# Linear attention with a gated causal convolution: gated values of three batches held, output chunks kept within a batch

## The chip, the core and the metric

The kernel runs on one core of one Trainium2 chip. The metric is the device time of one launch in microseconds, lower is better. Everything is computed in float32; the three weights arrive as float64 and are narrowed on the core.

## The reference

```python
# q, k, v: (8, 8, 576, 64); g_norm: (64,); w_val, w_out: (512, 512); conv_w: (5, 512)
kv  = einsum('bhsd,bhse->bhde', k, v)
out = einsum('bhsd,bhde->bhse', q, kv)
x   = out / sqrt(mean(out*out, -1) + 1e-6) * g_norm
x   = x.transpose(0, 2, 1, 3).reshape(8, 576, 512)
gate_pre = sum(conv_w[t] * xp[:, t:t+576] for t in range(5))   # xp: x with 4 zero tokens ahead
gate = 1 / (1 + exp(-gate_pre))
result = (gate * (x @ w_val)) @ w_out                           # (8, 576, 512)
```

## The kernel before

The work goes batch by batch. For each batch of 576 tokens there are these stages, each made of small steps:

- Loads on SP's queue: `load_half` brings k and v, each in two halves of 512 KB (tiles k0, k1, v0, v1) for 512 tokens; `load_tails` brings the last 64 tokens of both; `load_q` brings q in four parts, each by four DMAs (batches 0 and 1: `load_q_rows`, three parts). Tiles k0, k1, v0 and v1 have two buffers each and q has four.
- `kv_product` sums k by v of each head on PE with 64 stationary columns, alternating between the two halves of a bank; `kv_copy` brings the result to `kvbd`.
- q is turned: on PE and ACT for batches 0 and 1 (`turn_q_rows`, `sort_q`), on DVE for later ones (`turn_q`, which frees the buffer of that part of q).
- `raw_product` makes the attention output in chunks of 128 tokens (the last of 64), ACT squares it (`square`), DVE sums (`sums`, tile `ss`), POOL takes the power -1/2 (`powers`, tile `rt`), DVE multiplies (`normalise`, tile `x`).
- x is turned to channels by tokens (`xT`): on PE and ACT for batches 0 and 1 (`turn_x`, `keep_x`), by DVE blocks and POOL's DMAs for later ones (`turn_blocks`, `move_blocks`). `halo` fills the four tokens ahead.
- Gates: ACT starts (`gate_start`), four taps on DVE (`gate_tap`), a sigmoid on ACT (`gate_end`), for each of four groups of channels.
- Values: `val_product` for batches 0 to 3; for batches 4 to 7 `val_fast`, seven products of half size in place of eight, with sums by `x_sums`, `val_sums` and `val_keep`. The results go to the tile `gv`, and `gated` multiplies the gate into them.
- Outputs: two batches are a pair `i` with 1152 tokens in `gv`, which are nine chunks of 128. Chunks are taken two at a time, `p` = 0 to 3, as seven products of half size (`fast_product`, with `token_sums` and `weight_sums` on DVE, `fast_keep` on ACT and DVE). `single` plans the ninth chunk, which is the last 128 tokens of the pair's second batch, with four matmuls of 512 columns (`out_product`, `keep_out`). `store` writes each chunk by four DMAs on SP's queue from one of three `ot` buffers.

In `gv` there is room for two batches, batch `b` at tokens `b % 2 * 576`. So in pair `i` the outputs with `p` = 0 and 1 use tokens 0 to 511, all of the first batch, and `p` = 2 and 3 use tokens 512 to 1023, of both batches.

The order of the instructions on each engine is fixed when the program is built. Each step is given to a `Planner` with an engine, a duration, a wanted time, the results it needs, and rings of buffers that it takes and frees. The planner always places the step that can start first, by its own durations; each engine runs its steps in this order and waits for what they need. A wanted time is `want` plus an entry of the table `SHIFTS`, a hand of time per kind of step and batch. `by_batch` rings, `gv` among them, are taken in the order of the batches. `narrow_weight` steps narrow each weight in slices (5 on DVE, 3 on ACT) out of the ring `w64`; `keep_warm` puts small matmuls on an identity into PE's gaps in the first 60 us of the plan.

```python
"k0": 2, "k1": 2, "v0": 2, "v1": 2, "tails": 2, "q": 4, ... "gv": 2, "ot": 3,
...
t = step["want"] - step["ahead"]
...
key = (max(t, now), step["want"], step["at"])
```

Of the kernel before, what the change touches and what calls it, by code (L numbers as in the profile page):

```python
# [9 lines left out]
FP32 = mybir.dt.float32  # L10
# [8 lines left out]


SHIFTS = {
    "fast_keep": {2: -131.5},
    "fast_product": {0: 9, 1: 19.5, 2: -23, 3: -0.5},
    "gate_start": {6: 11},
    "gate_tap": {1: 52.5, 2: 75, 3: 66, 4: 61.5, 5: 66.5, 6: 72, 7: 72},
    "halo": {5: 35},
    "keep_out": {1: 24},
    "kv_product": {6: 43.5},
    "load_half": {("k", 4): -9, ("k", 6): -68, ("v", 1): 15, ("v", 4): 7.5, ("v", 5): 18.5, ("v", 6): 14.5,
        ("v", 7): 20.5},  # L30
    "load_q": {3: -18, 4: 21.5, 5: 3, 6: -8, 7: 3.5},
    "load_q_rows": {1: 30},
    "load_tails": {3: 12.5},
    "move_blocks": {6: 43},
    "narrow_weight": {("wout", 1): -35, ("wout", 3): -172.5, ("wval", 3): 17},
    "normalise": {5: 12, 6: 12, 7: -28},
    "raw_product": {4: 1, 5: 6, 6: -15, 7: -18.5},
    "sort_q": {1: -88},
    "stage_weight": {("cw", 0): -273.5, ("wout", 0): 13, ("wout", 1): -186.5, ("wval", 0): -297.5,
        ("wval", 2): -5},  # L40
    "sums": {4: 48},
    "turn_blocks": {4: 36.5},
    "turn_q": {2: 36.5, 3: 16.5, 6: 9.5},
    "turn_q_rows": {1: 5.5},
    "turn_x": {1: 55.5, 7: -7},
    "val_fast": {5: -9, 7: 12},
    "val_product": {0: 3, 1: 54.5},
    "val_sums": {3: 32.5},
    "weight_sums": {2: 28},
}  # L50


# [85 lines left out]
def kernel(  # L138
# [50 lines left out]
    HB = P // TB  # L189
    NV = 2  # L190
    SV = S // NV
    S2 = 2 * S
    TURNED = 2
    TURNED_X = 2
    FAST_VAL = range(4, B)
    GATES = 3
    assert NJ == 4 and NB == 18
    assert 2 * T == P and NB * TB == S and SV <= 512 and C <= 512 and D == 2 * TB

# [6 lines left out]
    def ps(kind, shape, name):  # L206
        return psum.tile(shape, FP32, tag=kind, bufs=BANKS[kind], name=name)

    plan = Planner({
        "k0": 2, "k1": 2, "v0": 2, "v1": 2, "tails": 2, "q": 4, "w64": 3, "y": 1, "wexp": 2,  # L210
        "kv": 1, "kvbd": 2, "qT": 2, "tp": 1, "raw": 2, "mm": 4, "sq": 2, "ss": 3, "rt": 3,
        "x": 2, "xT": 2, "gate": GATES, "xs": 4, "gv": 2, "ot": 3,
    }, by_batch=("tails", "kvbd", "xT", "gv"))


# [3 lines left out]
    ident = const.tile([P, P], FP32, name="ident")  # L219
    mhalf = const.tile([P, H], FP32, name="mhalf")  # L220
    xTs = [const.tile([P, NK, SX], FP32, name=f"xT{i}") for i in range(2)]
    gv = const.tile([P, NK, S2], FP32, name="gv")

    sqs = [const.tile([P, H, D + 1], FP32, name=f"sq{i}") for i in range(2)]
    squared = []
# [30 lines left out]
    st = {}  # L256

    def load_half(name, src, b, i):
        t = loads.tile([P, H // 2, NJ, D], FP32, tag=f"{name}{i}", name=f"{name}{i}_{b}")
        nc.sync.dma_start(  # L260
            out=t[:].rearrange("p h j d -> p h (j d)"),
            in_=src[b, i * H // 2:(i + 1) * H // 2, 0:SF, :].rearrange(
                "h (p j) d -> p h (j d)", j=NJ),
        )
        st[name, b, i] = t
# [4 lines left out]
                out=tails[b % 2][n][0:T], in_=src[b, :, SF:S, :].rearrange("h s d -> s h d"))  # L270

    def load_q(b, hp):
        t = loads.tile([P, NB, D], FP32, tag="q", bufs=4, name=f"q{b}_{hp}")
        run = S // TB * D - TB
        flat = t[:].rearrange("p n d -> p (n d)")
        for half in range(2):
            for r in range(2):
                first = (2 * r + half) * TB
                nc.sync.dma_start(
                    out=flat[first:first + TB, 0:run],  # L280
                    in_=q[b, 2 * hp + r].rearrange("(t n) d -> t (n d)", t=TB)[
                        :, half * TB:half * TB + run],
                )
        st["q", b, hp] = t

    def load_q_rows(b, i):

        t = loads.tile([P, NB, D], FP32, tag="q", bufs=4, name=f"q{b}_{i}")
        t = t[:].rearrange("p n d -> p (n d)")
        if i < 2:  # L290
            t = t[:, 0:H // 2 * NJ * D]
            nc.sync.dma_start(
                out=t.rearrange("p (h a) -> p h a", h=H // 2),
                in_=q[b, i * H // 2:(i + 1) * H // 2, 0:SF, :].rearrange(
                    "h (p j) d -> p h (j d)", j=NJ),
            )
            st["q", b, i] = t.rearrange("p (h j d) -> p h j d", h=H // 2, j=NJ)
        else:
            t = t[0:T, 0:C].rearrange("p (h d) -> p h d", h=H)
            nc.sync.dma_start(out=t, in_=q[b, :, SF:S, :].rearrange("h s d -> s h d"))  # L300
            st["q", b, i] = t
# [287 lines left out]
        st["val", b, jt, n] = val  # L589

    def keep_val(b, jt, n):
        first = b % 2 * S + n * SV
        nc.scalar.copy(out=gv[:, jt, first:first + SV], in_=st["val", b, jt, n][:])  # L593

    def gated(b, jt):
        both = gv[:, jt, b % 2 * S:(b % 2 + 1) * S]
        nc.vector.tensor_tensor(out=both, in0=both, in1=st["gate", b, jt][:], op=ALU.mult)  # L597


# [37 lines left out]

    def val_keep(b, mj, n):
        a, b_, c = (st[bank, "val", b, mj][:] for bank in "abc")
        to = lambda o, half: gv[:, mj + 2 * o, b % 2 * S + half * SV:b % 2 * S + (half + 1) * SV]  # L640
        add = lambda out, one, two: nc.vector.tensor_tensor(out=out, in0=one, in1=two, op=ALU.add)
        if n == 0:
            nc.scalar.copy(out=to(0, 0), in_=a)
        elif n == 1:
            nc.scalar.copy(out=to(1, 1), in_=c)
        elif n == 2:
            nc.scalar.copy(out=to(0, 1), in_=a)
        elif n == 3:
            add(to(0, 0), b_, to(0, 0))
        elif n == 4:  # L650
            add(to(1, 1), a, to(1, 1))
        elif n == 5:
            add(to(0, 1), c, to(0, 1))
        else:
            nc.scalar.copy(out=to(1, 0), in_=a)

    rows_out = out.rearrange("b (t n) c -> b n t c", n=NB)

    def out_product(i, c):
        po = ps("mm", [P, C], f"out{i}_{c}")  # L660
        for jt in range(NK):
            nc.tensor.matmul(  # L662
                po[:], gv[:, jt, c * P:(c + 1) * P], wout[:, jt, :],
                start=(jt == 0), stop=(jt == NK - 1),
            )
        st["po", i, c] = po

    def keep_out(i, c):
# [11 lines left out]
    def token_sums(i, h, n):  # L680

        if n % 2 == 0:
            st["sums", i, h, n // 2] = loads.tile(
                [P, 2, NK // 2, 2, P], FP32, tag="w64", bufs=3, name=f"sums{i}_{h}_{n}")
        block = lambda r, k: gv[:, k, h * SF:(h + 1) * SF].rearrange(
            "p k (m r t) -> p k m r t", m=2, r=2)[:, :, :, r, :]
        new = st["sums", i, h, n // 2][:, n % 2]
        second = st["sums", i, h, 0][:, 1]
        one, two, op = (
            (block(1, EVEN), block(1, ODD), ALU.add),  # L690
            (st["sums", i, h, 0][:, 0], block(0, EVEN), ALU.subtract),
            (block(0, EVEN), block(1, EVEN), ALU.subtract),
            (block(0, ODD), second, ALU.subtract))[n]
        nc.vector.tensor_tensor(out=new, in0=one, in1=two, op=op)
# [5 lines left out]
    def fast_product(i, p, n):  # L700


        h, m = divmod(p, 2)
        chunk = lambda r, k: lambda: gv[:, k, (2 * p + r) * P:(2 * p + r + 1) * P]
        total = lambda s: lambda: st["sums", i, h, s // 2][:, s % 2, :, m, :]
        bank, tokens, weights_ = (
            ("a", chunk(0, EVEN), wout[:, EVEN, LOW]), ("c", total(0), wsum[:, 0]),
# [34 lines left out]
    def store(i, c):  # L742
        ot = st["ot", i, c]
        for j in range(HB):
            bb, n = divmod(c * HB + j, NB)
            nc.sync.dma_start(
                out=rows_out[2 * i + bb, n], in_=ot[j * TB:(j + 1) * TB, :])

# [207 lines left out]
    def single(b, first):  # L956
# [1 line left out]
        key = b // 2, 2 * NJ  # L958
        plan.add(
            "PE", 3.45, first, out_product, *key,  # L960
            needs=gated_all(b) + [("wout", jt) for jt in range(NK)] + [("fast", (b // 2, 3, 6))],
            gives=[("po", key)], takes=[("mm", ("po", key))], frees=[("gv", b)],
        )
        plan.add(
            "ACT", 0.5, first + 3.6, keep_out, *key, needs=[("po", key)], gives=[("ot", key)],
# [7 lines left out]
    def outputs(b, first):  # L973

        i, h = divmod(b, 2)
        used = gated_all(b - 1, b) if h else gated_all(b)
        for n in range(4):
            plan.add(
                "DVE", 0.62, first - 4.0 + n, token_sums, i, h, n,
# [3 lines left out]
        for m in range(2):  # L983
            p = 2 * h + m
            t = first + 6.2 * m
            for n in range(7):
# [9 lines left out]
                    + ([("wsum", 3)] if n not in (0, 3) else [("wout", jt) for jt in range(NK)]),  # L996
                    gives=[("fast", key)],
                    takes=[(out_bank(i, p), (bank, i, p)) for bank in ("cb", "a")] if n == 0 else [],
                    frees=([("gv", b - 1)] if n == 6 and p == 2 else [])
                    + ([("w64", ("sums", i, h, 0))] if n == 2 and m else [])  # L1000
                    + ([("w64", ("sums", i, h, 1))] if n == 5 and m else []),
                )
# [104 lines left out]

    with tc.manual_schedule():
        set_up()
        idle_from = 3.0  # L1110
        for start, step in plan.order():
            if step["engine"] == "PE" and start < 60.0:
                keep_warm(int((start - idle_from) / 0.3))
                idle_from = start + step["time"]
            step["fn"](*step["args"])
# [30 lines left out]
```

## Time and profile before

| what | us |
|---|---|
| median of 11 runs | 339.24 |
| lowest and highest | 337.61, 341.74 |
| the profiled execution | 340.19 |
| its span | 338.13 |
| busy: PE, DVE, ACT, POOL | 320.7, 279.6, 151.4, 137.4 |

The profile is of one execution; its time is 2.06 us above its span, which is what lies around the span. Times of instructions count from the start of the span. PE is TensorE's matmuls, DVE is VectorE, ACT is ScalarE, POOL is GpSimd, SP is SyncE, and SPq is the issue of DMAs by SP. A line such as L409 is a line of the kernel; `x20` is the number of records. A float32 matmul leaves two matmul records and two weight loads.

### The profile page before, as it was taken

What the parts mean: (1) busy time and instruction counts of PE and PEld (TensorE: products, weight loads), DVE (VectorE), ACT (ScalarE), POOL (GpSimd) and SP (SyncE); (2) the same over time, 40 slices, a digit from 0 to 9 for tenths busy, and PEclk for the clock granted to TensorE, in tenths of its full rate; (3) what the DMA queues carried; (4) which work ended last, traced back from release to release, by engine and by line L of the source; (5) the groups of instructions that cost most, each with busy time, mean ns of one, the idle gap of its engine ahead of it and who ended that gap; (6) DMA issues with size and microseconds to landing.
All of it is one profiled execution on the core that took longest, in us unless ns stands there. A gap on an engine that the chain in (4) does not pass through costs nothing.

```text
span 338.1 us, 6366 instructions
## 1 busy us (share of the span) xinstructions
PE 320.7 (95%) x2225; PEld 261.2 (77%) x2225; DVE 279.6 (83%) x504; ACT 151.4 (45%) x325; POOL 137.4 (41%) x178
## 2 busy tenths in 40 slices
PE   7889999859999999999999999999999999999994
PEld 7878877747878787778888877768878877688781
DVE  2426989999999869799998989899999998889620
ACT  4236887664324442526245424362354443425311
POOL 3006302363355945176286525950847265000000
PEclk9799999999999999999999999999999999999999
DMA  6999998868439847998974439964424225101223
GB/s 180 267 244 326 284 245 221 257 191 225 139 97 263 249 97 190 258 255 247 258 169 141 95 70 246 228 142 150 97 61 93 65 63 124 31 21 44 63 62 94
DMA packets 46014, 55.37 MB, mean 164 GB/s; under 512 B 15754, under 2 KB 36254, under 8 KB 45982
## 3 DMA queue, kind: packets, MB, share of 16 engines
q1 hardware_dynamic: 42750, 48.67, 55.7%
q0 software_dynamic: 3072, 6.30, 8.1%
q8 instruction: 17, 0.28, 0.4%
q14 instruction: 15, 0.12, 0.1%
q10 hardware_dynamic: 160, 0.00, 0.0%
HBM read 39.21 MB, written 9.44 MB: 144 GB/s over the span
## 4 chain that ended last, share of the span: by engine, by line
PE 63%; DMA 14%; DVE 8%; SPq 6%; POOL 4%; issue 3%; ACT 1%; DVEq 0%; POOLq 0%
PE a L717 13%; PE val L584 11%; PE cb L717 11%; PE raw L486 8%; PE va L634 7%; DMA q<-in_q_dram 4%; DMA xT<-y 4%; PE kv L409 4%; PE vc L634 3%; PE out L662 3%; DMA v<-in_v_dram 3%; SPq L260 3%; POOL rt L514 2%; PE vb L634 2%; SPq L269 2%
## 5 line engine op out<-in xcount | busy, mean ns | idle before, releaser
L514 POOL TENSOR_TENSOR rt<-ss,mhalf 128x8 f32<-128x8 f32 (+1 forms) x40 | 70.0, 1753 | 98.9 <-DVE ss L508 98.8
L572 DVE SCALAR_TENSOR_TENSOR gate<-xT,cwT,gate 128x576 f32<-128x576 f32 x128 | 98.2, 808 | 0.0
L555 POOL DMA_DIRECT2D xT<-y x96 | 52.9, 558 | 36.6 <-PE cb L717 10.6
L584 PE MATMUL val<-xT,wval 128*128 128x288 f32 x256 | 65.1, 409 | 0.7 <-ACT xT L539 0.7
L584 PEld LDWEIGHTS val<-xT,wval 128*128 128x128 f32 x256 | 48.0, 190 | 14.0 <-ACT xT L539 0.9
L486 PE MATMUL raw<-kvbd,qT 128*128 128x128 f32 (+1 forms) x320 | 39.1, 281 | 3.0 <-DVE x L522 3.0
L486 PEld LDWEIGHTS raw<-kvbd,qT 128*128 128x128 f32 (+1 forms) x320 | 35.2, 180 | 8.5 <-issue 2.8
L500 ACT ACTIVATE sq<-raw 128x512 f32<-128x512 f32 (+1 forms) x40 | 22.2, 554 | 36.4 <-PE raw L486 34.7
L508 DVE TENSOR_REDUCE ss<-sq 128x8 f32<-128x520 f32 (+1 forms) x40 | 25.3, 632 | 10.4 <-ACT sq L500 10.4
L717 PE MATMUL a<-wsum,sums 128*128 128x256 f32 x128 | 33.4, 383 | 0.1
L522 DVE TENSOR_TENSOR x<-raw,rt 128x512 f32<-128x512 f32 (+1 forms) x40 | 24.7, 624 | 4.8 <-POOL rt L514 4.6
L597 DVE TENSOR_TENSOR gv<-gv,gate 128x576 f32<-128x576 f32 x32 | 23.7, 751 | 3.7 <-ACT gate L579 2.5
L717 PEld LDWEIGHTS a<-wsum,sums 128*128 128x128 f32 x128 | 23.7, 190 | 3.9 <-ACT ot L732 0.5
L593 ACT COPY gv<-val 128x288 f32<-128x288 f32 x32 | 12.8, 399 | 31.0 <-PE val L584 30.9
L726 DVE TENSOR_TENSOR ot<-cb,ot 128x256 f32<-128x256 f32 x32 | 13.5, 422 | 13.3 <-DMA out_dram<-ot 4.2
L579 ACT ACTIVATE gate<-gate 128x576 f32<-128x576 f32 x32 | 21.5, 683 | 6.5 <-DVE gate L572 6.5
L566 ACT ACTIVATE gate<-xT,cwT 128x576 f32<-128x576 f32 x32 | 23.3, 771 | 0.9 <-DVE gv L597 0.8
L409 PEld LDWEIGHTS kv<-v,k 128*64 128x64 f32 x512 | 17.7, 138 | 4.8 <-issue 3.7
L409 PE MATMUL kv<-v,k 128*64 128x64 f32 x512 | 20.4, 225 | 0.7 <-DMA v<-in_v_dram 0.7
L398 PE MATMUL kv<-ident 128*128 128x128 f32 x96 | 17.0, 345 | 2.2 <-POOL ident masks.py:199 1.4
L634 PE MATMUL va<-xs,vsum 128*128 128x288 f32 x64 | 18.2, 407 | 0.0
L398 PEld LDWEIGHTS kv<-ident 128*128 128x128 f32 x96 | 15.6, 253 | 2.7 <-POOL ident masks.py:199 1.4
(106 smaller groups left out, 516.1 us busy)
## 6 DMA issues: line engine op xcount, KB each, us to landing
q<-in_q_dram SPq DMA_DIRECT2D x96, 140.0 KB, 5.0
out_dram<-ot SPq DMA_DIRECT2D x144, 64.0 KB, 1.7
k<-in_k_dram SPq DMA_DIRECT2D x16, 512.0 KB, 8.2
v<-in_v_dram SPq DMA_DIRECT2D x16, 512.0 KB, 7.8
xT<-y POOLq DMA_DIRECT2D x96, 64.0 KB, 2.9
w_wval<-in_moe_w_val_dram SPq DMA_DIRECT2D x4, 512.0 KB, 9.0
w_wout<-in_moe_w_out_dram SPq DMA_DIRECT2D x4, 512.0 KB, 8.1
q<-in_q_dram SPq DMA_DIRECT2D x4, 512.0 KB, 8.6
```

Of the source, the lines that this page charges most:

```text
L398: nc.tensor.matmul(st["spare"].rearrange("p h d -> p (h d)")[:, 0:P], ident[:], ident[:], start=True, stop=True)
L409: nc.tensor.matmul(kvp[r * D:(r + 1) * D, hp, :], st["k", b, half][:, h, j, :] if j < NJ else kl[:, 2 * hp + r, :], st["v", b, half][:, h, ...
L486: nc.tensor.matmul(raw[row * m:(row + 1) * m, col * P:(col + 1) * P], st["qT", b][:, hp, c * P:c * P + m], kv_bd[b % 2][:, hp, :], start=T ...
L508: nc.vector.reduce_sum(out=ss[:, 0:n], in_=st["sq", b, c][:, 0:n], axis=AX.X)
L514: nc.gpsimd.tensor_tensor(out=rt[:, 0:n], in0=st["ss", b, c][:, 0:n], in1=mhalf[:, 0:n], op=ALU.pow)
L522: nc.vector.tensor_tensor(out=x[:, 0:n * D].rearrange("p (h e) -> p h e", h=n), in0=st["raw", b, c][:, 0:n * D].rearrange("p (h e) -> p h ...
L555: nc.gpsimd.dma_start(out=xTs[b % 2][i * TB:(i + 1) * TB, :, first:first + P], in_=y[a * TB:(a + 1) * TB, i])
L572: nc.vector.scalar_tensor_tensor(out=gate[:], in0=xTs[b % 2][:, jt, tap * TB:tap * TB + S], scalar=cwT[:, tap, jt:jt + 1], in1=gate[:], op ...
L584: nc.tensor.matmul(val[:], wval[:, kc, jt * P:(jt + 1) * P], xTs[b % 2][:, kc, HALO + n * SV:HALO + (n + 1) * SV], start=(kc == 0), stop=( ...
L597: nc.vector.tensor_tensor(out=both, in0=both, in1=st["gate", b, jt][:], op=ALU.mult)
L634: nc.tensor.matmul(st[bank, "val", b, mj][:], weights_[:, k], tokens()[:, k], start=(n in (0, 1, 3) and k == 0), stop=(k == NK // 2 - 1), ...
L717: nc.tensor.matmul(st[bank, i, p], tokens()[:, k], weights_[:, k], start=(n < 2 and k == 0), stop=(k == NK // 2 - 1), skip_group_check=True)
```

## The change

- `gv` holds three batches, batch `b` at tokens `b % 3 * 576`, so the ring `gv` has three places.
- The chunk pairs of the outputs lie within a batch: `p` = 0 and 1 are the first 512 tokens of the pair's first batch, `p` = 2 and 3 those of the second. Their needs shrink to that one batch, and its place in `gv` is freed by them and by `single`.
- The ninth chunk is made of the last 64 tokens of both batches. `out_product` makes it with eight matmuls of 64 stationary columns, alternating between the two halves of the bank; it no longer waits for the last `fast_product`. `store` sends its rows to both batches.
- To make room, k1 and v1 have one buffer instead of two, and q has three instead of four.
- All entries of `SHIFTS` are new, and PE's first gap is counted from 9.0 instead of 3.0. So the planner's order changes on all engines: loads at the start are w_val's slices 3 and 2, both halves of v, q, the tails of batches 0 and 1, w_out's slice 3, then the halves of k; three of the four slices of w_out are narrowed later.

```diff
 SHIFTS = {
-    "fast_keep": {2: -131.5},
-    "fast_product": {0: 9, 1: 19.5, 2: -23, 3: -0.5},
...
+    "fast_product": {0: -31.5, 1: 1.5, 2: -4},
+    "gate_tap": {0: 13, 1: 77, 2: 43, 3: 77, 4: 87, 5: 70.5, 6: 69.5, 7: 67.5},
...
+    GVS = 3
...
-        "k0": 2, "k1": 2, "v0": 2, "v1": 2, "tails": 2, "q": 4, "w64": 3, "y": 1, "wexp": 2,
+        "k0": 2, "k1": 1, "v0": 2, "v1": 1, "tails": 2, "q": 3, "w64": 3, "y": 1, "wexp": 2,
...
-        "x": 2, "xT": 2, "gate": GATES, "xs": 4, "gv": 2, "ot": 3,
+        "x": 2, "xT": 2, "gate": GATES, "xs": 4, "gv": GVS, "ot": 3,
...
-    gv = const.tile([P, NK, S2], FP32, name="gv")
+    gv = const.tile([P, NK, GVS * S], FP32, name="gv")
...
     def gated(b, jt):
-        both = gv[:, jt, b % 2 * S:(b % 2 + 1) * S]
+        both = gv[:, jt, b % GVS * S:(b % GVS + 1) * S]
...
     def out_product(i, c):
         po = ps("mm", [P, C], f"out{i}_{c}")
         for jt in range(NK):
-            nc.tensor.matmul(
-                po[:], gv[:, jt, c * P:(c + 1) * P], wout[:, jt, :],
-                start=(jt == 0), stop=(jt == NK - 1),
-            )
+            for r in range(2):
+                first = (2 * i + r) % GVS * S + SF
+                nc.tensor.matmul(
+                    po[r * T:(r + 1) * T], gv[:, jt, first:first + T], wout[:, jt, :],
+                    start=(jt == 0), stop=(jt == NK - 1),
+                )
...
     def fast_product(i, p, n):
-        chunk = lambda r, k: lambda: gv[:, k, (2 * p + r) * P:(2 * p + r + 1) * P]
+        begin = (2 * i + h) % GVS * S + 2 * m * P
+        chunk = lambda r, k: lambda: gv[:, k, begin + r * P:begin + (r + 1) * P]
...
     def store(i, c):
-            bb, n = divmod(c * HB + j, NB)
+            bb, n = divmod(c * HB + j, NJ * HB) if c < 2 * NJ else (j // 2, NJ * HB + j % 2)
...
     def single(b, first):
-            needs=gated_all(b) + [("wout", jt) for jt in range(NK)] + [("fast", (b // 2, 3, 6))],
-            gives=[("po", key)], takes=[("mm", ("po", key))], frees=[("gv", b)],
+            needs=gated_all(b - 1, b) + [("wout", jt) for jt in range(NK)],
+            gives=[("po", key)], takes=[("mm", ("po", key))], frees=[("gv", b - 1), ("gv", b)],
...
     def outputs(b, first):
-        used = gated_all(b - 1, b) if h else gated_all(b)
+        used = gated_all(b)
...
-                    frees=([("gv", b - 1)] if n == 6 and p == 2 else [])
+                    frees=([("gv", b)] if n == 6 and m else [])
...
-        idle_from = 3.0
+        idle_from = 9.0
```

More of the change, by code (lines that the diff above doesn't have):

```diff
@@ L21 @@
 SHIFTS = {
-    "fast_keep": {2: -131.5},
-    "fast_product": {0: 9, 1: 19.5, 2: -23, 3: -0.5},
[L24 to L49, printed above, removed]
+    "fast_product": {0: -31.5, 1: 1.5, 2: -4},
+    "gate_tap": {0: 13, 1: 77, 2: 43, 3: 77, 4: 87, 5: 70.5, 6: 69.5, 7: 67.5},
+    "keep_x": {0: -25},
+    "kv_product": {5: -4.5, 6: -4.5, 7: -10.5},
+    "load_half": {("k", 0): 7.5, ("k", 1): 13.5, ("k", 3): 6.5, ("k", 4): -7, ("k", 5): 34.5,
+        ("k", 6): 3.5, ("v", 0): -60.5, ("v", 1): 19.5, ("v", 2): 27.5, ("v", 4): 13, ("v", 5): -9.5,
+        ("v", 6): 3, ("v", 7): 9.5},
+    "load_q": {4: -11.5, 5: -12, 6: -14.5, 7: -11.5},
+    "load_tails": {4: 4.5, 5: -101.5, 6: -108.5},
+    "narrow_weight": {("wout", 0): 36, ("wout", 1): 20.5, ("wout", 3): -39},
+    "normalise": {7: 10.5},
+    "out_product": {1: 38.5, 3: -6},
+    "raw_product": {4: -84, 5: -23, 6: -17.5},
+    "square": {2: -9},
+    "stage_weight": {("cw", 0): -235.5, ("wout", 0): 13, ("wout", 1): 22, ("wout", 3): -4,
+        ("wval", 2): -117, ("wval", 3): -123.5},
+    "store": {0: 57.5},
+    "sums": {2: 9.5, 5: -91},
+    "token_sums": {0: 11.5},
+    "turn_blocks": {6: 23, 7: 9},
+    "turn_q": {2: 5.5, 3: 27.5},
+    "turn_x": {1: 3, 3: 7.5},
+    "val_fast": {7: 12.5},
+    "val_product": {0: 33.5, 1: 23, 3: 8.5},
+    "weight_sums": {0: 35.5},
+    "x_sums": {6: -9},
 }
@@ L191 @@
     SV = S // NV
-    S2 = 2 * S
     TURNED = 2
@@ L258, in load_half @@
     def load_half(name, src, b, i):
-        t = loads.tile([P, H // 2, NJ, D], FP32, tag=f"{name}{i}", name=f"{name}{i}_{b}")
+        t = loads.tile([P, H // 2, NJ, D], FP32, tag=f"{name}{i}", bufs=2 - i, name=f"{name}{i}_{b}")
         nc.sync.dma_start(
@@ L272, in load_q @@
     def load_q(b, hp):
-        t = loads.tile([P, NB, D], FP32, tag="q", bufs=4, name=f"q{b}_{hp}")
+        t = loads.tile([P, NB, D], FP32, tag="q", bufs=3, name=f"q{b}_{hp}")
         run = S // TB * D - TB
@@ L286, in load_q_rows @@
     def load_q_rows(b, i):
-        t = loads.tile([P, NB, D], FP32, tag="q", bufs=4, name=f"q{b}_{i}")
+        t = loads.tile([P, NB, D], FP32, tag="q", bufs=3, name=f"q{b}_{i}")
         t = t[:].rearrange("p n d -> p (n d)")
@@ L591, in keep_val @@
     def keep_val(b, jt, n):
-        first = b % 2 * S + n * SV
+        first = b % GVS * S + n * SV
         nc.scalar.copy(out=gv[:, jt, first:first + SV], in_=st["val", b, jt, n][:])
     def gated(b, jt):
-        both = gv[:, jt, b % 2 * S:(b % 2 + 1) * S]
+        both = gv[:, jt, b % GVS * S:(b % GVS + 1) * S]
         nc.vector.tensor_tensor(out=both, in0=both, in1=st["gate", b, jt][:], op=ALU.mult)
@@ L639, in val_keep @@
         a, b_, c = (st[bank, "val", b, mj][:] for bank in "abc")
-        to = lambda o, half: gv[:, mj + 2 * o, b % 2 * S + half * SV:b % 2 * S + (half + 1) * SV]
+        to = lambda o, half: gv[:, mj + 2 * o, b % GVS * S + half * SV:b % GVS * S + (half + 1) * SV]
         add = lambda out, one, two: nc.vector.tensor_tensor(out=out, in0=one, in1=two, op=ALU.add)
@@ L684, in token_sums @@
                 [P, 2, NK // 2, 2, P], FP32, tag="w64", bufs=3, name=f"sums{i}_{h}_{n}")
-        block = lambda r, k: gv[:, k, h * SF:(h + 1) * SF].rearrange(
+        begin = (2 * i + h) % GVS * S
+        block = lambda r, k: gv[:, k, begin:begin + SF].rearrange(
             "p k (m r t) -> p k m r t", m=2, r=2)[:, :, :, r, :]
```

## The prediction

> **What bounds the kernel now.** I read the page's busy shares first, then busy time by stage, then the chain of waits, then the order of instructions on PE, DVE and SP near the places that the change touches.
>
> ```profile
> PE 320.7 (95%) x2225; PEld 261.2 (77%) x2225; DVE 279.6 (83%) x504; ACT 151.4 (45%) x325; POOL 137.4 (41%) x178
> ```
>
> PE is nearly always busy, but "busy" holds fillers and slow stretches, so I count its work. From the chain's rows: a matmul of 288 columns takes 0.485 us (0.97 for two), of 256 columns 0.43, of 512 columns 0.86 (3.43 for the four of a tail chunk), `raw` 0.217, a half-wide `kv` matmul 0.066. With 240, 224, 16, 128 (and 32 half-wide at 0.12), 320, 48 transposes at 0.15 and 80 turns of q at 0.12, that is 116.4 + 96.9 + 13.7 + 31.5 + 21.0 + 7.2 + 9.6 = 296 us. PE's last matmul ends at 333.1, so 37 us go elsewhere. Where?
>
> ```profile
> 27.10:73.90 46.80, 42.30 (x433) 34.99 (x431) 42.95 (x74) 35.14 (x72) 19.30 (x18) 1.00 1.00 265
> 73.90:117.80 43.90, 42.31 (x360) 35.10 (x360) 40.84 (x74) 18.81 (x40) 23.45 (x25) 1.00 0.67 184
> 117.80:220.00 102.20, 101.33 (x635) 82.78 (x631) 92.28 (x163) 42.67 (x92) 58.13 (x76) 1.00 0.76 188
> 220.00:333.10 113.10, 112.22 (x557) 87.30 (x555) 95.25 (x162) 44.12 (x95) 33.95 (x51) 1.00 0.31 79
> ```
>
> (Columns: stage; its length; busy PE, PE loads, DVE, ACT, POOL; granted clock; DMA share; GB/s.) Until 73.9 DVE is the full engine (42.95 of 46.8) and PE has done only 48 us of its 296. From then on PE is full, and DVE close behind until 117.8.
>
> ```profile
> 12.61 10.23 DMA v<-in_v_dram
> 22.98 1.40 PE kv L409 x40
> 26.13 4.37 PE raw L486 x40
> ...
> 233.41 1.31 PE kv L409 x40
> 234.72 1.06 PE a L717 x4
> 235.78 0.86 PE cb L717 x4
> ...
> 240.10 0.73 PE kv L409 x20
> 240.83 1.06 PE a L717 x4
> ```
>
> The chain starts with a load: batch 0's last half of v is issued at 12.61 and lands at 22.84, and `raw` of batch 0 follows at 26.1. Later it is PE almost alone. See the price of a change between full and half-wide matmuls: the first `a` after `kv` takes 1.06 instead of 0.86, and a lone `kv` of 20 records takes 0.73, where two in one take 1.31. That is 0.20 us leaving and 0.075 us entering. With 58 such changes in PE's order, 8.0 us of the 37 go there.
>
> **The change, part by part.** Instruction counts are from the built orders of both programs. Sums are made against the profiled execution (340.19 us, span 338.13, PE's last matmul at 333.1). It is 0.95 us above the median of 339.24; I add the difference to the median.
>
> *Last tokens in two halves.* Four times, 4 matmuls of 512 columns (3.43 us) become 8 with 64 stationary columns, each pair writing two halves of one bank. If halves of a pair run together, the cost is near zero; one behind the other, 3.43 x 4 = +13.7 us. Nearest row:
>
> ```profile
> 14.38 3.71 PE L447 MATMUL qTps<-ident,q 128*64 128x128 f32 x64
> ```
>
> These 32 matmuls (two records each) have the same shape of weights, alternate halves of a bank, and take 0.116 us each; full-wide ones over the same 128 columns take 0.217. So pairs overlap. I take +0.02 us a pair, 0.3 us in all. But mode changes come with it. The Trainium skill, TensorEngine Tiling (Array Packing), Key Properties, says that changing the tiling mode drains the engine. The page gives no number; by its other statement alone (tiles operate independently) this edit would be free, while the rows above price a change pair at 0.275 us. The rows decide.
>
> *Mode changes.* In the changed program's order PE changes between full and half-wide 76 times, not 58: eight for the four tail chunks, ten because `kv` of later batches is cut by more output steps. 9 pairs x 0.275 = +2.5 us. Nothing hides this while PE is the full engine; 4.5 us of the 10.4 fall behind the outputs of batch 1.
>
> *Start: load order.* SP issues in order. From the sixth load of 512 rows on it is held back and issues one each 1.4 us (row below), landing 9 to 10 us later.
>
> ```profile
> 11.16 1.41 SPq L260 DMA_DIRECT2D k<-in_k_dram  x1
> ```
>
> Ahead of the load that completes `kv` of batch 0, the new order puts three more such loads: a second slice of w_val and the tails of batch 1. That is 4.2 us, less about 0.75 since the held-back stage begins at 4.8 instead of 5.55: the last k is issued near 16.1 where the last v now is at 12.61, so `kv` and `raw` of batch 0 come 3.5 us later, `raw` near 29.6.
>
> *Start: weights moved.* DVE's queue from the first `ss` to `x` of batch 1, chunk 0, falls. Start-to-start from the rows: taps 0.735, 512-wide operations 0.60, short narrowing steps 0.34, gated 0.67, transposes 0.62 + 0.13. Before: 31 x 0.60, 16 x 0.735, 11 x 0.34, 5 x 0.65, 4 x 0.67, small ones 2.0 = 42.1 us. After: 25 x 0.60, 16 x 0.735, 5 x 0.34, 2 x 0.65, 4 x 0.67, four q transposes 3.0, small ones 1.3 = 36.7 us. One slice of w_out is narrowed before `raw`, the others behind `x`. In the trace:
>
> ```profile
> 27.18 0.42 DVE L508 TENSOR_REDUCE ss<-sq 128x4 f32<-128x260 f32 x1 [6.41 <-ACT sq L500]
> ...
> 73.17 0.68 DVE L522 TENSOR_TENSOR x<-raw,rt 128x512 f32<-128x512 f32 x1
> ```
>
> First `ss` at 30.6 + 36.7 + 3 of idle (3.85 now) = 70.3 for that `x`, against 73.8. But PE must be there too. With POOL's powers 1.7 us apart, `x` of batch 0 ends near 40; turns of q of batch 1 stand ahead of the first `val`, which starts near 42.6; from it to the transpose of that `x` lie 27.4 us of work, 1.1 of mode changes and about 1 of waits: 72, against 73.99 in the trace. Gain: 2.0 us, mode changes so far included. Its cover: if q of batch 1 lands later than 38, PE loses it one for one.
>
> *Three batches of gv.* The products of batch 2 no longer wait for the outputs of batch 1's pair; in the new order one stands ahead of batch 0's last output steps and three more ahead of batch 1's outputs. So when the first output of batch 1 starts, PE has done 96.8 us of work instead of 87.6. That is the tightest place for DVE: in the trace it starts at 117.87, and DVE's last gated value of batch 1 is done at 116.9. In the new order, DVE's sums need 49.4 us behind that `x`, plus about 2 of idle: 70.3 + 51.4 = 121.7. PE needs 72 + 49.2 + 1.7 mode changes + 1.9 waits (1.65 now) = 124.8. DVE is clear by 3 us, PE is the limit, and the gain of 2.0 us is kept, not enlarged.
>
> *From there to the end.* Work left 199.5, mode changes 4.7, waits 3.75 as now (PE's end 333.1 less 117.87 less 208.7 of work less 2.75 changes), plus 0.3 for the pairs: 124.8 + 208.25 = 333.1. The same as now: later mode changes give the 2.0 us back.
>
> *Fewer load buffers.* q has 3 buffers, the second halves of k and v one. Such a half loads only after the last `kv` of the batch before. Bound: zero if it lands in time; all 6 later batches late by 2 us, 12 us. Nearest rows: two v halves together land in 5.3 to 5.9 us in mid-run, four in 8.2. Tightest: v of batch 4 is queued on SP behind the stores of the first two chunks, whose last copy comes near 104; issued at 105.5, landed 111 to 113.7, wanted by PE near 114. Others have 4 us or more. I take 0.
>
> *End.* Now the tail chunk is last: PE ends at 333.1, one copy of 0.58, four stores.
>
> ```profile
> 304.88 30.63 SPq L746 DMA_DIRECT2D out_dram<-ot  x31
> ...
> 329.50 3.60 PE L662 MATMUL out<-wout,gv 128*128 128x512 f32 x8
> ...
> 333.18 0.58 ACT L670 COPY ot<-out 128x512 f32<-128x512 f32 x1 [3.11 <-DMA out_dram<-ot]
> ```
>
> SP's last issue ends at 335.5. In the new order the last pair's two chunks finish together behind the tail chunk: eight stores of 0.43 us instead of four, minus the shorter copy: +1.1 us. The tail chunk's 3.4 us also let buffers of `ot` drain, where PE waited 0.5 us: -0.4.
>
> *Sum.* Start -2.0; later mode changes and pairs +2.0; end +0.7: 340.19 + 0.7 = 340.9, or **340.0 us** on the median.
>
> **The rivals.**
>
> 1. *The start gains more.* If loads issue faster (the first 5 us of SP cost 0.4 to 0.7 us each), `raw` is late by 2 us only and waits of PE shrink to DVE's limit, the gain at batch 1's outputs is 4.5 to 5 us: 337. For: DVE's margin of 3 us. Against: DMA share is 1.00 through the start.
> 2. *Slower: v of batch 4 late.* It decides once v takes over 8.6 us to land, as the loads of the start do. PE would wait 2 to 3 us at that `kv`, with everything behind it in order, and a further 1 us where the halves of k of batch 5 come behind q of batch 6: 343.5. For: three q buffers chain SP to DVE's transposes. Against: DMA share is 0.67 there.
> 3. *Slower: the halves of a pair don't overlap* with 512 columns: +13.7, 353. The row above is against it.
> 4. *The change does not do what it says in time*: the orders differ everywhere, but both are PE-full after 74, so 339.2.
>
> **How the numbers follow.** A measurement of this kernel can tell about 0.3%, 1.0 us, from no change. Chances: this sum 0.46 (its own range 337.8 to 342), rival 1 0.22, rival 2 0.24, rival 3 0.04, rival 4 0.04. The sum's centre, +0.75, lies inside the 1.0 us, so its chances split 0.10 faster, 0.16 same, 0.20 slower. With rival 1 nearly all faster (0.21 and 0.01 same), rival 2 slower but for 0.01 each, rival 3 slower and rival 4 same: 0.32, 0.22, 0.46. The range 336.5 to 344.5 leaves out rival 3, the best part of rival 1 and the worst of rival 2.
>
> **What would show it.** Right: `raw` of batch 0 near 29.6; the transpose of batch 1's last `x` near 72; the first output of batch 1 near 125; each tail chunk 3.4 to 3.7 us, with the first full-wide matmul behind it 0.2 us longer; eight stores behind the last matmul. Wrong: PE waiting on DMA at `kv` (rival 2), tail chunks near 6.9 us (rival 3), PE at the first output of batch 1 by 122 (rival 1).

## The result and the profile after

The changed kernel takes 337.61 us (median of 13 runs, 336.99 to 338.41); the kernel before, run beside it, 339.51. The ratio is 0.9945, 95% interval 0.9925 to 0.9965: faster by 1.9 us. The forecast was 340.0 with a range of 336.5 to 344.5 and a slowdown as the likelier sign. The time lies in the range, but the sign was wrong. The profiled execution took 337.79 us, its span 336.0; that of the kernel before took 340.19, so the two profiles differ by 2.4 us, 0.5 more than the medians.

The page's busy shares, and then busy time by stage (stage; length; busy PE, PE loads, DVE, ACT, POOL; granted clock; DMA share; GB/s), the first two cut at the places that answer to those of before:

```profile
PE 319.3 (95%) x2251; PEld 256.7 (76%) x2251; DVE 281.9 (84%) x504; ACT 151.7 (45%) x325; POOL 140.1 (42%) x178
```

```profile
27.40:70.20 42.80, 42.74 (x440) 35.80 (x440) 38.39 (x66) 30.14 (x64) 20.84 (x18) 1.00 0.87 245
70.20:121.70 51.50, 50.65 (x409) 42.36 (x408) 49.23 (x90) 25.71 (x54) 26.87 (x30) 1.00 0.87 222
121.70:220.00 98.30, 97.97 (x626) 76.55 (x627) 90.64 (x158) 40.92 (x88) 58.00 (x75) 1.00 0.71 191
220.00:330.00 110.00, 108.79 (x552) 84.24 (x548) 91.49 (x153) 40.72 (x90) 31.73 (x46) 1.00 0.26 63
```

The first stage is where the two differ most. It is 42.8 us long and PE is busy for 42.7 of them; before, it was 46.8 long, PE had 42.3 and DVE was the full engine. The shares of the whole span (95% both times) show none of this.

The waits of PE from the first value product to the first output of batch 1, first of the kernel before (36 to 117.8 us), then of the changed one (42 to 121.7 us); the columns are total us, times, longest:

```profile
PE raw L486 <- DVE x L522: 2.3, 3, 1.1
PE xTps L532 <- DVE x L522: 2.1, 2, 1.8
PE xTps L532 <- ACT xT L539: 0.7, 1, 0.7
PE val L584 <- ACT xT L539: 0.7, 1, 0.7
```

```profile
PE raw L484 <- DVE x L520: 0.8, 1, 0.8
```

That is 5.8 us against 0.8: the 5.0 us saved here are the source of the gain, and what the new order costs elsewhere is paid out of them. DVE, on which most of these waits were, gets from its first `ss` of batch 0 to batch 1's last `x` in 40.0 us, where it took 46.0 (27.18 to 73.17):

```profile
28.51 0.42 DVE L506 TENSOR_REDUCE ss<-sq 128x4 f32<-128x260 f32 x1 [2.25 <-ACT sq L498]
...
68.54 0.66 DVE L520 TENSOR_TENSOR x<-raw,rt 128x512 f32<-128x512 f32 x1
...
120.03 0.65 DVE L520 TENSOR_TENSOR x<-raw,rt 128x512 f32<-128x512 f32 x1
```

The last of these rows is the `x` for which PE still waits 0.8 us, just ahead of batch 1's first output. The marks that the prediction named, in PE's order of time of the changed kernel:

```profile
42.26 2.21 PE L582 MATMUL val<-xT,wval 128*128 128x288 f32 x8
...
70.15 0.60 PE L530 MATMUL xTps<-ident,x 128*128 128x128 f32 x4
...
120.74 1.16 PE L484 MATMUL raw<-kvbd,qT 128*128 128x128 f32 x8 [0.77 <-DVE x L520]
121.73 1.03 PE L720 MATMUL a<-wout,gv 128*128 128x256 f32 x4
...
209.59 3.65 PE L663 MATMUL out<-wout,gv 128*64 128x512 f32 x16
213.17 1.24 PE L632 MATMUL va<-xs,wval 128*128 128x288 f32 x4
...
329.13 1.03 PE L720 MATMUL a<-wsum,gv 128*128 128x256 f32 x4
```

The first value product starts at 42.3; the transposition of batch 1's last `x` at 70.2; batch 1's first output at 121.7, with 9.2 us more of work behind PE than before; a tail chunk takes 3.65 us, and the full-wide row behind it is 0.1 us longer than its like (1.24 for 1.13); the last matmul ends at 330.2. The chain of waits at the start:

```profile
4.11 2.62 SPq L290
...
9.62 1.66 SPq L267
11.32 1.47 SPq L267
12.83 1.42 SPq L267
...
14.37 1.37 SPq L309
15.78 6.64 DMA k<-in_k_dram
...
22.56 1.39 PE kv L407 x40
...
27.46 2.57 PE raw L484 x24
```

As the prediction said, the last k is issued near 16 us (15.78). But it lands 6.64 us later and not 9 to 10, so `raw` of batch 0 starts 1.3 us later than before (26.13) and not 3.5. This landing is one of several: in six profiles of the runs below whose start is the same, `raw` starts between 26.8 and 28.2.

### The profile page after: what moved, and what is told of

It reads as the page before. It is cut to its first block, busy times and chain, and to the rows that moved or that the text cites. A ratio compares the mean times of both kernels' runs of the same rounds, so it can differ in the third digit from the quotient of the medians.

```text
span 336.0 us, 6403 instructions
## 1 busy us (share of the span) xinstructions
PE 319.3 (95%) x2251; PEld 256.7 (76%) x2251; DVE 281.9 (84%) x504; ACT 151.7 (45%) x325; POOL 140.1 (42%) x178
## 4 chain that ended last, share of the span: by engine, by line
PE 85%; DVE 5%; SPq 4%; DMA 2%; issue 1%; ACT 1%; DVEq 0%; ACTq 0%
PE val L582 19%; PE a L720 14%; PE cb L720 12%; PE raw L484 10%; PE va L632 9%; PE kv L407 6%; PE vc L632 4%; PE out L663 4%; PE vb L632 2%; DMA k<-in_k_dram 2%; PE xTps L530 2%; SPq L267 2%; DVE gate L570 2%; PE qTps L445 1%; SPq L290 1%
## 5 line engine op out<-in xcount | busy, mean ns | idle before, releaser
L512 POOL TENSOR_TENSOR rt<-ss,mhalf 128x8 f32<-128x8 f32 (+1 forms) x40 | 71.0, 1785 | 100.2 <-DVE ss L506 100.0
L553 POOL DMA_DIRECT2D xT<-y x96 | 52.8, 557 | 35.8 <-PE a L720 14.3
L720 PE MATMUL cb<-wout,sums 128*128 128x256 f32 x64 | 17.2, 391 | 0.6 <-DVE ot L729 0.2
L720 PE MATMUL cb<-wsum,sums 128*128 128x256 f32 x64 | 16.7, 385 | 0.3 <-DVE sums L696 0.3
```

The costliest lines, as they stand in the source:

```text
L512: nc.gpsimd.tensor_tensor(out=rt[:, 0:n], in0=st["ss", b, c][:, 0:n], in1=mhalf[:, 0:n], op=ALU.pow)
L553: nc.gpsimd.dma_start(out=xTs[b % 2][i * TB:(i + 1) * TB, :, first:first + P], in_=y[a * TB:(a + 1) * TB, i])
L720: nc.tensor.matmul(st[bank, i, p], tokens()[:, k], weights_[:, k], start=(n < 2 and k == 0), stop=(k == NK // 2 - 1), skip_group_check=True)
```

## The experiments

Each time is a median beside runs of the kernel before on the same chip. Ratios are to that kernel; the changed kernel's own is 0.9945.

### What the third batch of gated values is worth

Edit, in the changed kernel's planner:

```diff
-        "x": 2, "xT": 2, "gate": GATES, "xs": 4, "gv": GVS, "ot": 3,
+        "x": 2, "xT": 2, "gate": GATES, "xs": 4, "gv": 2, "ot": 3,
```

> The changed kernel, but the planner may hold gated values of two batches only: its order is the changed kernel's up to raw_product of batch 4, chunk 3; from there batch 2's first product waits for batch 0's tail chunk, so PE has done 88 us of work ahead of the first output of batch 1 and not 96.8. Theory (the third batch lets PE run ahead of DVE): DVE's last gated value of batch 1 comes near 118.8 (119.4 in the changed kernel), PE would be there near 113.2 and waits some 5 us for it; time 341 to 343. Rival (the shorter DVE queue at the start gives the gain by itself, the third batch nothing): no wait over 1 us ahead of batch 1's outputs, time 337 to 338.5.

And the reverse, the kernel before with nothing but the new table `SHIFTS` in place of its own, and the fillers' start:

```diff
-        idle_from = 3.0
+        idle_from = 9.0
```

> The kernel before with the changed kernel's table of shifts and its start of the fillers, and nothing else of the change: two batches of gated values, pairs across batches, tail chunk of 128 tokens, all load buffers. Its start is nearly the changed kernel's, PE has 88 us of work ahead of batch 1's outputs, PE changes mode 54 times against 76. Theory (the gain needs the third batch): PE waits for DVE ahead of batch 1's outputs, which start near 119, and the time is 339 to 341, no faster than before. Rival (the table makes the gain): 335.5 to 337.5.

Measured: 360.93 us with two batches (ratio 1.0647, 1.0604 to 1.069), and 348.14 with the table alone (1.0261, 1.0209 to 1.0313). In both, the theory of the third batch had the sign right, but the losses are far larger than I expected. PE's order of time with the table alone:

```profile
112.89 0.29 PE L407 MATMUL kv<-vl,kl 128*64 128x64 f32 x4
118.52 1.12 PE L484 MATMUL raw<-kvbd,qT 128*64 128x128 f32 x8 [5.34 <-DVE x L520]
119.58 2.08 PE L715 MATMUL a<-wout,gv 128*128 128x256 f32 x4
121.44 1.92 PE L484 MATMUL raw<-kvbd,qT 128*128 128x128 f32 x8
123.15 1.66 PE L715 MATMUL cb<-wsum,sums 128*128 128x256 f32 x4
124.65 1.03 PE L715 MATMUL a<-wsum,sums 128*128 128x256 f32 x4
```

PE is through with what it has ahead of batch 1's outputs at 113.1, some 5 us sooner than in the kernel before (117.9). So the new start does give PE a lead: its waits from batch 0's first value product to 113 us come to 1.0 us, which means that the new table alone takes most of them away. But then PE's order has nothing more to put there: batch 2's products need the place in `gv` that batch 1's pair still holds. PE waits 5.34 us for DVE, whose queue is about where it is in the changed kernel (the `x` that PE waits for, below, starts there at 118.14):

```profile
117.69 0.68 DVE L520 TENSOR_TENSOR x<-raw,rt 128x512 f32<-128x512 f32 x1
```

So what the third batch gives is 9.2 us of work that PE can do while DVE gets to this place. And PE pays again for the wait: an output row of 1.03 us takes 2.08, the next two rows 1.92 and 1.66 instead of 1.05 and 1.03, in all 2.6 us more. Busy time in the wait and behind it (columns as above) shows DVE full, and the granted clock at half:

```profile
113.20:118.50 5.30, 0.00 (x0) 0.01 (x1) 5.30 (x9) 3.42 (x6) 1.39 (x1) 0.92 0.65 160
118.50:123.15 4.65, 4.63 (x20) 3.96 (x21) 4.65 (x9) 1.90 (x5) 1.01 (x2) 0.50 0.88 268
```

The Trainium skill, TensorE: Matmul & The Clock Gate, Part 1, says that the clock falls to half after an idle window of about 3.4 us and is full again after as long a busy one. This trace agrees: in narrower stretches the clock is at half from about 117.6, 4.4 us into the wait, to about 124.4. By the wait alone this place would cost 5.3 us, with the clock it costs 7.9.

With two batches and the changed kernel's pairs the same happens several times over:

```profile
116.78 0.70 PE L720 MATMUL a<-wout,gv 128*128 128x256 f32 x2 [3.14 <-DVE gv L595]
120.00 3.13 PE L484 MATMUL raw<-kvbd,qT 128*64 128x128 f32 x16 [2.51 <-DVE x L520]
...
148.54 2.08 PE L720 MATMUL cb<-wout,sums 128*128 128x256 f32 x4 [3.45 <-ACT ot L733]
150.41 1.81 PE L720 MATMUL a<-wsum,gv 128*128 128x256 f32 x4
152.05 13.26 PE L582 MATMUL val<-xT,wval 128*128 128x288 f32 x54
```

At 152.05 it starts on work that the changed kernel reaches at 136.3, about 110 us of PE's work in both: 15.7 us of the 23 are lost by then. The rest comes later. How much of either loss belongs to the missing batch, and how much to a table that was drawn for three and orders the steps badly for two, these runs can't split. What they show is that this table's new start only pays with the third batch; a table drawn for two was not tried, nor were the edits with the old table.

### How much DVE has to spare

Edit: behind 4, or 8, of batch 0's taps one addition on a tile that nothing else uses.

```diff
+    steps[n] = start, dict(step, fn=lambda *a: (gate_tap(*a), nc.vector.tensor_tensor(
+        out=spare[:], in0=spare[:], in1=spare[:], op=ALU.add)))
```

> The changed kernel with four idle additions of 512 values (0.60 us each) put into DVE's queue behind taps of batch 0's gates, between 44 and 60 us: 2.4 us more of DVE work in the stretch that ends at batch 1's outputs. In the changed kernel DVE's last gated value of batch 1 ends at 119.5 and PE comes for it at 121.7, 2.2 us later. Theory (PE is the limit from 42 us on, DVE has 2 us to spare): no more than 0.5 us longer, 337.5 to 338.2. Rival (DVE is the limit, its idle microseconds only look like slack): the 2.4 us come out whole, 340.

> The same with eight such additions, 4.8 us more of DVE work. Theory: the 2.2 us of slack are used up and about half comes out: 339.5 to 341, with PE waiting on DVE between 60 and 122 us (in the changed kernel 0.8 us). If DVE never limits PE there: 337.6. If DVE is the limit throughout: 342.4.

Measured: 338.43 us with four (0.9972, 0.9952 to 0.9993), 340.41 with eight (1.0032, 1.0016 to 1.0049). So 2.4 us of DVE work cost 0.8, and 4.8 cost 2.8 against the changed kernel: the first 1.6 to 2 us are free, what comes after is paid in full. PE's waits with eight, from the first gates to batch 1's outputs:

```profile
58.05 1.16 PE L486 MATMUL raw<-kvbd,qT 128*128 128x128 f32 x8 [0.77 <-DVE x L522]
...
73.27 0.63 PE L532 MATMUL xTps<-ident,x 128*128 128x128 f32 x4 [0.82 <-DVE x L522]
...
123.88 1.16 PE L486 MATMUL raw<-kvbd,qT 128*128 128x128 f32 x8 [0.77 <-DVE x L522]
124.88 1.03 PE L722 MATMUL a<-wout,gv 128*128 128x256 f32 x4
```

Two of the three waits are new, and of the kind that the kernel before had in this stretch. In this profile the first output of batch 1 is 3.15 us later than in the changed kernel (124.88 for 121.73). 0.7 of that is a later landing of k, the other 2.4 are all lost by the row at 73.27; the list shows 1.6 of them as waits. This is the direct test: such waits come back as soon as DVE's queue is nearly as long again as it was. It does not account for all of the 5.0 us, since the changed order of PE's own steps was not tested apart. At batch 1's first output nothing more is lost: there PE and DVE are later by the same time, and the wait of 0.77 stays what it was. The theory stands; its 0.5 us for four additions was somewhat low.

### Slots or bytes in the load queue

Edit: `load_tails` of batch 1 is moved from ahead of batch 0's two halves of k to just behind them.

> The changed kernel with the loads of batch 1's tails (two of 128 KB) moved on SP from ahead of batch 0's two halves of k to just behind them. Theory of slots (the prediction's: a held-back load costs 1.4 us whatever its size): k of batch 0 lands 2.8 us earlier, raw of batch 0 near 24.6, time 335 to 337. Theory of bytes (what lands is set by the bytes queued ahead at about 349 GB/s): 0.25 MB less ahead, k lands 0.75 us earlier, raw near 26.7, time 336.9 to 337.6.

Measured: 336.74 us (0.9922, 0.9897 to 0.9947), 0.9 below the changed kernel. In the listing of DMA issues (KB each, median us to landing) the two k of batch 0, first in the changed kernel, where they are issued from 15.78 on, then with the tails behind, from 12.91 on:

```profile
k<-in_k_dram SPq DMA_DIRECT2D x2, 512.0 KB, 7.2
```

```profile
k<-in_k_dram SPq DMA_DIRECT2D x2, 512.0 KB, 8.8
```

Issued 2.9 us sooner, they take 1.6 us longer, so they land 1.3 us sooner, against 2.8 by slots and 0.75 by bytes. `raw` starts 1.1 us sooner (26.38 in the chain, 27.46 in the changed kernel), but that is no measure of the landing, since PE doesn't wait for k in this run. The small matmuls of `keep_warm` (fillers, L396) end at 21.56 and the key-value products follow at once:

```profile
19.58 1.98 PE kv L396 x16
21.56 1.31 PE kv L407 x40
```

In the changed kernel PE had 1.1 us of waiting for k behind the same fillers, so no more could be gained here. And landings scatter: where the start is unchanged, the listing gives 6.7 to 8.2 us for these two loads from run to run. So this test doesn't decide between slots and bytes. The 1.1 us that `raw` gains are not hidden anywhere: PE's transposition of batch 1's last `x` comes 1.0 us sooner, its first output of batch 1 as well.

### What a change of mode costs

Edit: the planner's order is taken as it is, and for batches 5 to 7 the first three key-value products are moved to just ahead of the fourth.

```diff
+        for b in range(5, B):
+            at = places(kv_product, b)
+            moved = [steps[n] for n in at[:-1]]
+            for n in reversed(at[:-1]):
+                del steps[n]
+            steps[at[-1] - len(moved):at[-1] - len(moved)] = moved
```

> The changed kernel with the four key-value products of each of batches 5, 6 and 7 put together at the place of the last of them: PE changes between full and half-wide 62 times, not 76; nothing else moves on any engine. Theory (each pair of changes costs 0.275 us of a full PE): seven pairs fewer, 1.9 us less, 335.7. Rival (DVE, busy 91 of 98 us in that stretch, takes over, or a pair costs only near 0.1): 337.0 to 337.6.

Measured: 336.62 us (0.9916, 0.9885 to 0.9947), 1.0 less than the changed kernel and half of what was expected. The two `raw` rows enclose batch 6's four products, in the changed kernel apart and here together:

```profile
175.18 1.75 PE L484 MATMUL raw<-kvbd,qT 128*64 128x128 f32 x16
...
194.19 0.66 PE L484 MATMUL raw<-kvbd,qT 128*64 128x128 f32 x8
```

```profile
175.27 1.75 PE L484 MATMUL raw<-kvbd,qT 128*64 128x128 f32 x16
...
186.64 1.16 PE L484 MATMUL raw<-kvbd,qT 128*128 128x128 f32 x8 [0.36 <-DVE x L520]
...
193.87 0.66 PE L484 MATMUL raw<-kvbd,qT 128*64 128x128 f32 x8
```

The way between them is 19.01 us with four groups, 18.60 with one, though a new wait of 0.36 for DVE stands in it: 0.77 us for three pairs of changes, 0.26 each. The price of the prediction (0.275) is right. Of what the seven pairs save, two new waits for DVE took some back (this one and 0.24 us later on): a likely reason is that a key-value product between two other steps had been time in which DVE caught up. This profile's load also came 0.4 us later.

### Halves that don't alternate

Edit in the tail chunk: the loop over the two batches is put outside the loop over `jt`.

> The changed kernel with the two loops of the tail chunk exchanged: four products of batch 2i, then four of batch 2i+1, so that matmuls on the two halves of PE no longer stand side by side. Theory (only neighbours in the queue overlap): a tail chunk takes near 6.9 us instead of 3.6, four of them 13 us, 350. Rival (the halves run ahead of each other freely): 3.6 us each, 337.6.

Measured: 344.50 us (1.0149, 1.0124 to 1.0173), 6.9 more than the changed kernel. In PE's order of time:

```profile
211.06 5.42 PE L663 MATMUL out<-wout,gv 128*64 128x512 f32 x16
```

5.42 us instead of 3.65, four times: 7.1 us, which is the whole difference. Each record is as long in both (0.60 us). So it is the alternating order that makes the new tail chunk nearly free. The expected 6.9 us a chunk, the price of eight full-wide matmuls, was too much: eight in a row on the same half cost less than that estimate, and no run here shows why.

### The end, and the buffers

Edit for the end: the last chunk's four stores on ACT's queue.

```diff
-            nc.sync.dma_start(
+            queue = nc.scalar if (i, c) == (B // 2 - 1, 2 * NJ - 1) else nc.sync
+            queue.dma_start(
```

> The changed kernel with the four stores of the very last chunk issued by ACT, not by SP; the other chunk of the pair stays on SP. Theory (behind the last copy, at 330.6, eight issues of 0.43 us in one queue end at 333.4): ACT's four end near 332.3, 1.1 us less, 336.5. Rival (the transfers themselves, or a first issue on ACT, set the end): 337.3 to 337.8.

Measured: 336.68 us (0.9926, 0.9903 to 0.9949), 0.9 less. The last issues, first of the changed kernel, then here:

```profile
329.79 3.59 SPq L749 DMA_DIRECT2D out_dram<-ot  x8
```

```profile
329.18 1.73 SPq L750 DMA_DIRECT2D out_dram<-ot  x4
330.00 1.86 ACTq L750 DMA_DIRECT2D out_dram<-ot  x4
```

In the changed kernel SP issues until 333.4, 3.2 us behind the last matmul; here SP is done at 330.9 and ACT at 331.9, 2.3 us behind the last matmul, which in this profile ends 0.6 us sooner for an earlier start. From the last matmul to the end of the span it is 4.9 us instead of 5.8.

Edit for the buffers: the second half of v has two buffers again.

> The changed kernel with the second half of v in two buffers again, nothing else moved: undoes the part of the buffers' cut that was held tightest (v of batch 4). Theory (the cut costs nothing, all loads land in time): 337.3 to 338.0. Rival (a load that starts earlier spares PE a wait at the key-value product): 335.5 to 336.8.

Measured: 337.77 us (0.9976, 0.9955 to 0.9998). It gains nothing; the cut of this one buffer costs nothing that this run shows. One half of k and q's fourth buffer were not given back.

### The three gains together

> The changed kernel with the three edits that each gained near 0.9 us: tails of batch 1 behind batch 0's k, key-value products of batches 5 to 7 grouped, last chunk's stores on ACT. They act at the start, in the middle and behind the last matmul. If they add up: 337.6 - 0.9 - 1.0 - 0.9 = 334.8. If DVE, with about 2 us to spare at batch 1's outputs and 91 busy of 98 us behind them, swallows one: 335.7.

Measured: 334.58 us (0.9893, 0.9867 to 0.9918). This version is faster than both kernels, and by the times the three gains add up: 3.0 us, against 2.8 one by one. The kernel before was itself faster beside this run and the one before it (338.47, against 339.3 to 339.5 beside the others), so by the ratios it is 1.8 us against 2.4. The intervals allow either.

## Why the prediction was wrong, point by point

The prediction's sum, laid beside what the profile after shows (of single profiles, so the miss is 3.1 us; by the medians, 340.0 against 337.6, it is 2.4):

| stretch | predicted | measured |
|---|---|---|
| start to `raw` of batch 0 | 29.6 | 27.4 |
| to the first value product | 13.0 | 14.9 |
| to the transposition of batch 1's last `x` | 29.4 | 27.9 |
| to the first output of batch 1 | 52.8 | 51.6 |
| to PE's end | 208.25 | 208.4 |
| behind it, with what lies around the span | 7.8 | 7.6 |
| all | 340.9 | 337.8 |

- *Start, load order.* The issue was predicted right, the landing was not: 9 to 10 us were carried over, and it took 6.6. Why is open. Four of the loads ahead of k are of 128 KB, where the kernel before had two ahead of its v; each costs SP as much as one of 512 KB (1.4 to 1.7 us of issue) and is a quarter of the bytes, but the tails' run doesn't show that this is the reason. Missed: 2.2 us.
- *From there to the first value product* I had DVE's and POOL's chain set the pace. But PE is full there, with batch 1's key-value products and its turns of q, which the new order puts into this place, and with fillers of `keep_warm`: 14 records at 32.6, 35.6 and 36.4, about 2 us. The stretch is 1.9 us longer than predicted; no run left the fillers out. Together the first two rows miss by 0.3 only. That is luck: had `raw` come at 29.6, PE would have been as full behind it and everything 2.2 us later. The run with eight additions shows it, where `raw` came 0.7 us later and the first value product as well, and so does the tails' run, where what `raw` gained was passed on one for one.
- *Weights moved: the step that failed.* The prediction saw DVE's queue fall by 5.4 us up to batch 1's last `x` (measured, with its idle time: 6.0), and yet allowed PE "about 1 of waits" up to that place and "1.9 waits (1.65 now)" behind it. It took the waits of the kernel before as PE's own. Most of them were DVE's lateness, and with DVE's queue shorter they go as well: 0 and 0.8 us are left. The first stretch came out 1.5 us shorter (about 0.6 of it because its work and mode changes were reckoned too long), the second 1.2. This is most of the rest of the 3.1 us. The additions on DVE show the cause: put 4.8 us back, and waits on `x` return, and 2.8 us with them.
- *Three batches of gv.* The prediction had "PE is the limit" at batch 1's first output, with DVE "clear by 3 us", and so hardly priced the third batch ("kept, not enlarged"). That follows from the same step: without the waits PE is there first. It waits 0.77 us for DVE's `x`, which ends at 120.7, although DVE's last value of batch 1 is done at 119.5. The output starts at 121.7, which is the prediction's own sum for DVE. The runs with two batches show that without the third place this table's lead is lost whole at batch 1's outputs, and more.
- *From there to the end*, with *mode changes* and *pairs of halves*: 208.4 for 208.25. The price of a pair of changes measured 0.26 for 0.275; a tail chunk 3.65 us for "3.4 to 3.7". The stretch does give back some 2 us of the lead, as predicted: 2.4 of 5.3 (9.2 us more work done at batch 1's first output, 3.9 us later).
- *Fewer load buffers*: 0, as predicted; PE's only wait for a DMA at a key-value product is the one at the start.
- *The end*: eight stores at the end, as predicted, though the sum for them (+1.1) took off the whole of the last copy, 0.58, and not what the new copy is shorter (0.37). From the last matmul to the last issue it is 3.2 us for 2.4, since the first store starts 0.4 us ahead of that matmul's end. A second queue takes 0.9 us away.

Rival 1 is nearly what happened: "`raw` is late by 2 us only" (1.3), "waits of PE shrink to DVE's limit" (0.8 left, on DVE), batch 1's outputs "by 122" (121.7), 337 (337.6). Only its reason did not come true: the loads were not issued faster, they landed sooner. It was given 0.22, for the reason that the DMA share was 1.00 through the start. That share was no argument: it says that the engines are busy, not that the load that is waited for stands at the end of their queue. Rivals 2 to 4 did not occur.

## What to carry to other kernels

A wait of the busiest engine belongs to the engine that it waits for. When a change shortens that engine's queue, take the wait out of the sum, and keep only what the second engine's slack, worked out to the same place, still forces. A lead is only worth what the leading engine may do with it: ask at the next meeting point which work is allowed to stand ahead, and count the buffers that decide it. And before landing times are carried to a new order of loads, count what stands ahead of the load in bytes as well as in issues: here the two counts gave 0.75 and 2.8 us for a gain of 1.3.

## What the hardware showed that I had not expected

- Two long waits of PE were paid about half as much again: behind 5.34 us idle the next three rows took 2.6 us more than their like, behind 3.45 us (two batches, 148.54) the next two 1.8 more, at a granted clock of 0.50 and 0.51.
- Eight matmuls with 64 stationary columns over 512 columns take 3.65 us when the halves alternate and 5.42 when they don't: that is about halfway between four full-wide ones (3.4) and eight (6.9, estimated from their 0.86 each).
- ACT's queue issued four stores in 1.86 us right behind its copy, hardly slower than SP's 1.73 for four.
